# One attention-and-mixer kernel: v of the first batch placed in the mirror buffers, first loads spread by need, and one more batch fully mirrored by DMA

## The chip, the cores and the metric

One core of one Trainium2 chip. Times are device microseconds of a whole launch. A "span" is the profiled execution alone and is some 2 us shorter than the launch time of the same run. In the profiles PE is TensorE, PEld its weight loads, ACT ScalarE, DVE VectorE, POOL GpSimd and SPq the queue in which SyncE issues transfers; L396 is a line of the kernel.

## The reference, cut to what matters

```python
# B, S, D = 8, 3008, 256; z has 64 features
scores = (1 / S) * z @ z.T                 # symmetric in query and key
out    = maximum(scores, 0)**2 @ v
x      = u * out
h      = maximum(x.T @ w_tok1, 0) @ w_tok2   # token mixer, w_tok1 is 3008 x 256
y      = x + h.T
result = y + maximum(y @ w_ch1, 0) @ w_ch2   # channel mixer, 256 -> 1536 -> 256
```

Because scores are z times its own transpose, block (query q, key g) of the squared scores is the transpose of block (g, q). There are 6 x 6 blocks of 512 x 512 for each batch.

## The kernel before

A Python scheduler orders all instructions. TensorE computes score blocks ("sc"), ScalarE evicts them with a ReLU into one of six score buffers ("at"), VectorE squares them there, TensorE multiplies them with v ("acc"), VectorE gates with u into xT. The mixers follow ("a_ps", "h_ps", "hp", "op") and fill TensorE between attention blocks of the next batch. Batch 0 has no mixer work beside it.

A block that is not computed is a mirror: a DMA transpose of the score buffer into one of ten buffers "fl", issued from SyncE. The score buffer is free only when TensorE and that transpose have read it.

```python
def direct_block(b, q, g):           # computed on TensorE, not mirrored
    return b == 0 or g >= q or (b == 1 and g == 0)

def flips(b, q, g):                  # this computed block is also turned into (g, q)
    return g > q and not direct_block(b, g, q)

def flip(b, q, g, at, uses, done):
    fl = sb.tile([P, GK, QW], BF16, tag="fl", name="fl", bufs=ROOM["fl"])     # 10
    nc.sync.dma_start_transpose(
        out=fl.rearrange("p j (i s) -> p (j i) s", s=P), in_=at[:])
    blocks[b, g, q] = (done, fl[:, :, :], "fl", [1])
    release("at", uses, done.t)      # the score buffer: its last use may be the transpose
```

GpSimd issues the loads in program order, SyncE the transposes in program order; both stand still while the next one's buffer or data is not ready:

```python
def load_v(b, c):
    vt = sb.tile([P, GK, D], BF16, tag="v", name="v_sb", bufs=8)
    # ... (cut) one or three loads from GpSimd
def load_u(b, q):
    ur = sb.tile([P, QW // P, D], BF16, tag="ur", name="ur", bufs=2)
    # ... (cut) load from GpSimd
def turn_u(b, q):                    # uT, needed by the gate of block q
    # ... (cut) nc.sync.dma_start_transpose(out=uT, in_=ur)

# ... (cut) group n is the n-th attention block; v of the next batch near the end of this one
at_group(base + (NQ - 1) * NG - 2 + (j if j > 1 else 0), lambda b=b, c=c: load_v(b + 1, c))
for c in range(NG):
    at_group(NG - 1 + 4 * c, lambda c=c: load_w_tok1(c))
    at_group(NG + 1 + 4 * c, lambda c=c: load_w_tok2(c))
    at_group(NG + 4 + 4 * c, lambda c=c: order_w_tok2(c))
```

A group number orders the load in GpSimd's program.

Of the kernel before, what the change touches and what calls it, by code (L numbers as in the profile page):

```python
# [13 lines left out]
P = 128  # L14
# [4 lines left out]
class Done:  # L19


    def __init__(self, t=None):
        self.t = t


class Op:
# [16 lines left out]
def kernel(  # L43
# [100 lines left out]
                wp[:], zero[:, :P], zero[:], start=True, stop=True, skip_group_check=True)  # L144

    def load_v(b, c):
        vt = sb.tile([P, GK, D], BF16, tag="v", name="v_sb", bufs=8)
        n = full_tiles[c]
        nc.gpsimd.dma_start(out=vt[:, :n, :], in_=rows_of(v[b], c))  # L149
        if n < GK:  # L150
            for r in range(2):
                nc.gpsimd.dma_start(
                    out=vt[r * TAIL:(r + 1) * TAIL, n, :], in_=last_rows(v[b]))
        vs[b, c] = vt
        loading(LOAD)

    def load_u(b, q):
        ur = sb.tile([P, QW // P, D], BF16, tag="ur", name="ur", bufs=2)
        n = full_tiles[q]
        nc.gpsimd.dma_start(out=ur[:, :n, :], in_=rows_of(u[b], q))  # L160
        if n < QW // P:
            nc.gpsimd.memset(ur[TAIL:, n, :], 0.0)
            nc.gpsimd.dma_start(out=ur[:TAIL, n, :], in_=last_rows(u[b]))
        urs[b, q] = ur
        loading(LOAD)
# [18 lines left out]
        loading(LOAD)  # L184

    def load_w_tok2(c):
        st = sb.tile([P, DT, QW], BF16, tag="ws", name="ws", bufs=1)
        W = widths[c]
        nc.gpsimd.dma_start(
            out=st[:, :, :W],  # L190
            in_=moe_w_tok2.rearrange("(tc t) s -> t tc s", t=P)[:, :, c * QW:c * QW + W])
        ws[c] = st
        loading(LOAD)

    def order_w_tok2(c):
        st = ws.pop(c)
        W, n = widths[c], full_tiles[c]
        for h in range(DT):
            nc.gpsimd.tensor_copy(
                w_tok2_sb[:, h, c * QW:c * QW + n * P].rearrange("p (t s) -> p t s", s=P),  # L200
                st[:, h, :n * P].rearrange("p (s t) -> p t s", t=n))
        if n * P < W:
            nc.gpsimd.tensor_copy(
                w_tok2_sb[:, :, c * QW + n * P:c * QW + W], st[:, :, n * P:W])
# [18 lines left out]

    def direct_block(b, q, g):


        return b == 0 or g >= q or (b == 1 and g == 0)

    def flips(b, q, g):

# [286 lines left out]
    def finished(blk, g):  # L517
        blk.parts[g] -= 1
        if not blk.parts[g]:
            _, _, name, uses = blocks.pop((blk.b, blk.q, g))  # L520
            release(name, uses, pe[0] + 0.2)

    def block_ready(blk, g):
        e = blocks.get((blk.b, blk.q, g))
# [69 lines left out]
    def gate(blk, dh, t):  # L594
        b, q, W = blk.b, blk.q, blk.W
        acc = blk.acc[dh]
        uT = uTs[b, q]
        if dh == 0:
            xTs[b, q] = sb.tile([P, DT, QW], BF16, tag="xT", name="xT", bufs=ROOM["xT"])
            live["xT"] += 1  # L600
            live["x"] += 1
            if W < QW:
                nc.gpsimd.memset(xTs[b, q][:, :, W:], 0.0)
        xT = xTs[b, q]
        full, rest = W // P, W % P
        nc.vector.tensor_mul(  # L606
            xT[:, dh, :full * P].rearrange("p (t s) -> p t s", s=P),
            acc[:, :full * P].rearrange("p (t s) -> p t s", s=P),
            uT[:, :full, dh, :])
        if rest:  # L610
            nc.vector.tensor_mul(
                xT[:, dh, full * P:W], acc[:, full * P:W], uT[:, full, dh, :rest])
        if dh == DT - 1:
            push("sp", t, 1.25, 5.5, lambda t: turn_x(b, q, t), first=1)

    def turn_x(b, q, t):
        x = sb.tile([P, DT, QW // P, P], BF16, tag="x", name="x_sb", bufs=ROOM["x"])
# [19 lines left out]
    def add_mixer(b):  # L637
# [95 lines left out]
                release("xT", xT_uses[q])  # L733

        def ch2(q, half, i, end):
            if i == 0:
                take_slot()
                st["op"] = psum.tile([P, 2, D], F32, tag="ps", name="op", bufs=3)
            op = st["op"]
            n = full_tiles[q]  # L740
            both = half * 2 + i == n
            c0 = (half * 2 + i) * P
            for cc in range(CHT):
                if both:
                    h2 = pair["hs"][:, cc, :]
                else:
                    h2 = st["h2", q, cc // 2][:, cc % 2, c0:c0 + P]
                nc.tensor.matmul(  # L748
                    op[:, i, :], h2, w_ch2_sb[:, cc, :], start=(cc == 0 and i == 0),
                    stop=(cc == CHT - 1), skip_group_check=True)  # L750
            if i < pieces_of(q, half) - 1:
                return
            if half == halves(q)[1]:
                live["h2"] -= CHT // 2

            def residual(t):
                us = st["u", q]
                res = sb.tile([P, 2, D], F32, tag="res", name="res", bufs=3)
                if half * 2 + 1 < n:
                    nc.vector.tensor_add(  # L760
                        res.rearrange("p i (h d) -> p i h d", d=P),
                        op.rearrange("p i (h d) -> p i h d", d=P),
                        us[:, :, half * 2:half * 2 + 2, :].rearrange("p h i d -> p i h d"))
                    nc.sync.dma_start(
                        out=rows_of(out[b], q)[:, half * 2:half * 2 + 2, :],
                        in_=res[:])
                else:
                    k = half * 2
                    ends = [(0, slice(0, P), us[:, :, k, :], rows_of(out[b], q)[:, k, :])]
                    if i == 1:  # L770
                        lower, upper = slice(0, TAIL), slice(TAIL, P)
                        ends.append((1, lower, pair["ut"][:], last_rows(out[b - 1])))
                        ends.append((1, upper, us[upper, :, k + 1, :], last_rows(out[b])))
                    for j, r, u_rows, to in ends:
                        nc.vector.tensor_add(
                            res[r, j, :].rearrange("p (h d) -> p h d", d=P),
                            op[r, j, :].rearrange("p (h d) -> p h d", d=P), u_rows)
                        nc.sync.dma_start(out=to, in_=res[r, j, :])
                free["sp"] = max(free["sp"], t) + 0.4
                if half == halves(q)[1]:  # L780
                    live["us"] -= 1
            ring.append(push("dve", max(end + 0.21, known(st["turned", q])), 0.62, 0.75,
                             residual))
# [17 lines left out]
        def pieces_of(q, half):  # L801

            return 1 if q == NQ - 1 and half == 1 and b % 2 == 0 else 2

        def add_ch2(q, half, i):
            two = pieces_of(q, half) == 2
            tails.append(Piece(1.312, [h2_done[q, c2] for c2 in range(CHT // 2)] + w_done[2:],
                               lambda end: ch2(q, half, i, end), opens=two and i == 0,
                               closes=two and i == 1))

# [46 lines left out]

    vorder = [0, LAST] + list(range(1, LAST))
    new_zT(0)
    zero = sb.tile([P, QW], BF16, tag="ws", name="zero", bufs=1)  # L860
    nc.vector.memset(zero[:], 0.0)
    make_identity(nc, ident)
    zf0 = [first_z(c) for c in range(NG)]
# [24 lines left out]
    for b in range(B):  # L888
        base = b * NQ * NG
        for q in range(NQ):  # L890
            m = b * NQ + q + 2
            if m < B * NQ:
                at_group(base + q * NG + 2, lambda m=m: load_u(m // NQ, m % NQ))
                at_group(base + q * NG + 5, lambda m=m: turn_u(m // NQ, m % NQ))
        if b + 1 < B:
            held = {}

            def ask_z(b, c, held):
                held[c] = load_z(b + 1, c)

            at_group(base + 3 * NG, lambda b=b: new_zT(b + 1))
            for j, c in enumerate(vorder):
                at_group(base + 3 * NG + j, lambda b=b, c=c, h=held: ask_z(b, c, h))
                at_group(base + 3 * NG + j + 3, lambda b=b, c=c, h=held:
                         turn_next_z(b, c, h.pop(c)))
                at_group(base + (NQ - 1) * NG - 2 + (j if j > 1 else 0),
                         lambda b=b, c=c: load_v(b + 1, c))
    def turn_late_z(c):


# [16 lines left out]
        at_group(c - GK + 1, lambda c=c: turn_late_z(c))  # L927
    at_group(3, lambda: turn_u(0, 0))
    at_group(6, lambda: turn_u(0, 1))
    for c in range(NG):  # L930
        at_group(NG - 1 + 4 * c, lambda c=c: load_w_tok1(c))
        at_group(NG + 1 + 4 * c, lambda c=c: load_w_tok2(c))
        at_group(NG + 4 + 4 * c, lambda c=c: order_w_tok2(c))
    w_done = [Done() for _ in range(4)]

    def ask_w_ch(part):
        load_w_ch(part)
        w_done[part].t = pe[0] + 16.0

    for part in range(4):  # L940
        n = NG + 2 + 6 * part
        at_group(n, lambda part=part: ask_w_ch(part))

    per_batch = 0.87 * NQ * (2 + CHT // 2) + 1.35 * 4 * NQ
    flat = NQ * NG * 1.73 + NQ * (NQ + 1) / 2 * 0.63
# [130 lines left out]
```

## Time and profile before

| what | before |
|---|---|
| time, three runs | 1174.66 us (1174.34 to 1177.71) |
| its median in each of the five jobs of this record | 1174.5, 1172.22, 1172.69, 1172.89, 1173.0 |
| span; TensorE busy | 1170.1; 1162.0 us |
| score matmuls; groups of them in the timeline | 752; 130 |
| mirror transposes | 100 |

TensorE is the bound and has no gap above 0.21 us between 16 us and the last stage.

### The profile page before, as it was taken

How to read it: one execution, taken by the hardware profiler on the slowest of the kernel's cores; microseconds unless marked ns; L12 is line 12 of the kernel's file. 1: busy time of each engine (PE TensorE's matmuls, PEld its weight loads, DVE VectorE, ACT ScalarE, POOL GpSimd, SP SyncE). 2: the span in 40 equal slices, each digit the busy share in tenths (PEclk: the TensorE clock that was granted, in tenths of full speed). 3: DMA queues.
4: the chain of work that ended last, by engine and by line, in shares of the span. 5: the costliest groups of instructions: out<-in, count | busy, mean ns of one | idle time of the engine just before them, and what ended most of it. 6: DMA issues, size and time to landing. Idle time of an engine off the chain costs nothing.

```text
span 1170.1 us, 17839 instructions
## 1 busy us (share of the span) xinstructions
PE 1162.0 (99%) x7069; PEld 630.4 (54%) x7069; DVE 557.6 (48%) x836; ACT 523.4 (45%) x652; POOL 159.9 (14%) x328
## 2 busy tenths in 40 slices
PE   9999999999999999999999999999999999999998
PEld 3334455555546555464555655556454564555666
DVE  5776655355342653335534355332653337511544
ACT  7886644436342364434524245353544435433221
POOL 2561101200121110111101101011110110000000
PEclk9999999999999999999999999999999999999999
DMA  8997947989689985996969887798878989651232
GB/s 148 166 160 134 177 106 122 173 133 174 128 136 177 154 153 126 156 171 132 156 132 173 149 151 139 141 174 147 147 127 149 187 135 163 108 124 39 57 77 68
DMA packets 462339, 162.95 MB, mean 139 GB/s; under 512 B 426224, under 2 KB 439856, under 8 KB 462256
## 3 DMA queue, kind: packets, MB, share of 16 engines
q1 hardware_dynamic: 434400, 129.12, 59.0%
q0 software_dynamic: 27344, 32.32, 19.3%
q8 instruction: 55, 0.90, 0.3%
q10 hardware_dynamic: 512, 0.38, 0.1%
q14 instruction: 28, 0.23, 0.1%
HBM read 65.40 MB, written 24.64 MB: 77 GB/s over the span
## 4 chain that ended last, share of the span: by engine, by line
PE 97%; DMA 1%; DVE 1%; ACT 1%; issue 1%; SPq 0%; POOL 0%; DVEq 0%; ACTq 0%
PE acc L513 42%; PE op L748 21%; PE hp L707 21%; PE sc L379 7%; PE a_ps L653 4%; PE h_ps L670 3%; ACT at L417 1%; DMA zf<-in_z_dram 0%; DMA v_sb<-in_v_dram 0%; DVE xT L676 0%; DVE at L425 0%; DVE h2pre L722 0%; DVE xT L606 0%; SPq L120 0%; DVE res L760 0%
## 5 line engine op out<-in xcount | busy, mean ns | idle before, releaser
L417 ACT ACTIVATE at<-sc 128x1024 bf16<-128x1024 f32 (+1 forms) x294 | 280.9, 1023 | 205.2 <-PE sc L379 204.4
L513 PE MATMUL acc<-at,v_sb 128*128 128x512 bf16 (+2 forms) x1504 | 358.0, 378 | 0.6 <-DMA v_sb<-in_v_dram 0.5
L513 PEld LDWEIGHTS <-v_sb 128*128 128x128 bf16 (+1 forms) x2304 | 209.2, 97 | 268.2 <-issue 66.7
L720 ACT ACTIVATE h2pre<-hp 128x1024 bf16<-128x1024 f32 (+1 forms) x183 | 183.6, 1007 | 303.0 <-PE hp L707 300.3
L425 DVE TENSOR_TENSOR at<-at 128x1024 bf16<-128x1024 bf16 (+1 forms) x294 | 205.9, 708 | 170.3 <-ACT at L417 169.4
L707 PE MATMUL hp<-xT,w_ch_sb 128*128 128x512 bf16 (+1 forms) x1152 | 265.1, 375 | 0.0
L748 PE MATMUL op<-w_ch_sb,h2pre 128*128 128x256 bf16 x2208 | 258.4, 273 | 0.3 <-DVE xT L676 0.2
L748 PEld LDWEIGHTS <-h2pre 128*128 128x128 bf16 x2208 | 215.9, 98 | 46.2 <-issue 0.5
L513 PE MATMUL acc<-fl,v_sb 128*128 128x512 bf16 (+1 forms) x800 | 190.7, 371 | 0.2 <-DVE xT L606 0.2
L707 PEld LDWEIGHTS <-w_ch_sb 128*128 128x128 bf16 x1152 | 112.7, 98 | 126.7
L760 DVE TENSOR_TENSOR res<-op,u_sb 128x512 f32<-128x512 f32 x88 | 60.8, 691 | 209.2 <-PE op L748 206.2
L722 DVE TENSOR_SCALAR h2pre<-hp 128x1024 bf16<-128x1024 f32 (+1 forms) x105 | 126.5, 1205 | 54.3 <-PE hp L707 54.1
L606 DVE TENSOR_TENSOR xT<-acc,uT 128x512 bf16<-128x512 f32 (+1 forms) x96 | 63.3, 665 | 109.0 <-PE acc L513 108.7
L405 ACT ACTIVATE at<-sc 128x512 bf16<-128x512 f32 (+3 forms) x164 | 59.3, 447 | 87.5 <-PE sc L379 87.5
L379 PE MATMUL sc<-zT 64*128 64x512 bf16 (+1 forms) x752 | 97.8, 360 | 0.3
L453 DVE TENSOR_TENSOR at<-at 128x512 bf16<-128x512 bf16 (+3 forms) x164 | 47.0, 339 | 47.9 <-ACT at L405 47.9
L111 POOL COPY zr<-zs 128x512 bf16<-128x512 bf16 x42 | 26.5, 632 | 294.0 <-DMA zT<-zr 293.6
L379 PEld LDWEIGHTS <-zT 64*128 64x128 bf16 x752 | 32.0, 94 | 58.1 <-issue 40.0
L160 POOL DMA_DIRECT2D ur<-in_u_dram x48 | 25.9, 540 | 238.5 <-DMA uT<-ur 237.2
L676 DVE TENSOR_TENSOR xT<-xT,h_ps 128x1024 bf16<-128x1024 bf16 (+1 forms) x48 | 55.6, 1191 | 5.5 <-PE h_ps L670 5.5
L670 PE MATMUL h_ps<-w_tok_sb,a_sb 128*128 128x512 bf16 (+1 forms) x192 | 44.4, 374 | 0.1
L149 POOL DMA_DIRECT2D v_sb<-in_v_dram x48 | 25.9, 543 | 134.7 <-PE acc L513 134.5
(43 smaller groups left out, 228.1 us busy)
## 6 DMA issues: line engine op xcount, KB each, us to landing
out_dram<-res SPq DMA_DIRECT2D x88, 256.0 KB, 2.4
v_sb<-in_v_dram POOLq DMA_DIRECT2D x40, 256.0 KB, 4.9
ur<-in_u_dram POOLq DMA_DIRECT2D x40, 256.0 KB, 5.4
zs<-in_z_dram POOLq DMA_DIRECT2D x35, 64.0 KB, 4.5
at<-at SPq DMA_TRANSPOSE x123, 2.5
fl<-at SPq DMA_TRANSPOSE x100, 4.4
v_sb<-in_v_dram POOLq DMA_DIRECT2D x8, 192.0 KB, 7.3
w_ch_sb<-in_moe_w_ch_dram POOLq DMA_DIRECT2D x4, 384.0 KB, 5.7
```

The source lines that it names most:

```text
L379: nc.tensor.matmul(sc[:, r, c0:c1], zT[h, k * P:(k + 1) * P], zT[h, q * QW + c0:q * QW + c1], start=True, stop=True)
L405: nc.scalar.activation(a3[:, i, c0:c1], sc[:, r, c0:c1], ACT.Relu, scale=inv_S)
L417: nc.scalar.activation(view, sv, ACT.Relu, scale=inv_S)
L425: nc.vector.tensor_mul(view, view, view)
L513: nc.tensor.matmul(o, vs[blk.b, g][rows, i, dh * P:(dh + 1) * P], rhs, start=first, stop=stop, skip_group_check=True)
L606: nc.vector.tensor_mul(xT[:, dh, :full * P].rearrange("p (t s) -> p t s", s=P), acc[:, :full * P].rearrange("p (t s) -> p t s", s=P), uT[: ...
L670: nc.tensor.matmul(h[:, dh, :W], st["a"][:, th, dh * P:(dh + 1) * P], w_tok2_sb[:, th, q * QW:q * QW + W], start=(th == 0), stop=(th == 1))
L707: nc.tensor.matmul(hp[:, r, :W], w_ch1_sb[:, dc, cc * P:(cc + 1) * P], xT[:, dc, :W], start=(dc == 0), stop=(dc == DT - 1))
L720: nc.scalar.activation(h2[:, :, :W], hp[:, :, :W], ACT.Relu)
L722: nc.vector.tensor_single_scalar(h2[:, :, :W], hp[:, :, :W], 0.0, AX.max)
L748: nc.tensor.matmul(op[:, i, :], h2, w_ch2_sb[:, cc, :], start=(cc == 0 and i == 0), stop=(cc == CHT - 1), skip_group_check=True)
L760: nc.vector.tensor_add(res.rearrange("p i (h d) -> p i h d", d=P), op.rearrange("p i (h d) -> p i h d", d=P), us[:, :, half * 2:half * 2 + ...
```

## The change

Its intent: compute five score blocks less, in batch 1, and make room and DMA time for their mirrors. The core, with cuts marked:

```diff
 def load_v(b, c):
-    vt = sb.tile([P, GK, D], BF16, tag="v", name="v_sb", bufs=8)
+    if b == 0:
+        vt = sb.tile([P, GK, D], BF16, tag="fl", name="v_sb", bufs=ROOM["fl"])
+        live["fl"] += 1
+    else:
+        vt = sb.tile([P, GK, D], BF16, tag="v", name="v_sb", bufs=8)
 ... (cut)
-    ur = sb.tile([P, QW // P, D], BF16, tag="ur", name="ur", bufs=2)
+    ur = sb.tile([P, QW // P, D], BF16, tag="ur", name="ur", bufs=3)
 ... (cut: the staging tile of w_tok2 moves into the room of "h2")
-    return b == 0 or g >= q or (b == 1 and g == 0)
+    return b == 0 or g >= q
 ... (cut)
-    push("sp", t, 1.25, 5.5, lambda t: turn_x(b, q, t), first=1)
+    push("sp", t, 1.25, 7.5, lambda t: turn_x(b, q, t), first=1)
 ... (cut: the last pair of output pieces is added and stored in two halves)
-    tails.append(Piece(1.312, [h2_done[q, c2] for c2 in range(CHT // 2)] + w_done[2:],
+    needs = [Sooner(h2_done[q, c2], 0.218 * c2) for c2 in range(CHT // 2)]
+    tails.append(Piece(1.312, needs + w_done[2:],
 ... (cut)
+items = [lambda c=c: load_v(1, c) for c in vorder]
+items += [lambda c=c: load_w_tok1(c) for c in range(NG)]
+first_tok2 = len(items)
+items += [lambda c=c: load_w_tok2(c) for c in range(NG)]
+items += [lambda part=part: ask_w_ch(part) for part in range(4)]
+for k, item in enumerate(items):
+    n = NG - 2 + k * (NQ - 1) * NG // len(items)
+    at_group(n, item)
```

More of the change, by code (lines that the diff above doesn't have):

```diff
@@ L23, in __init__, with t @@
         self.t = t
+class Sooner:
+    def __init__(self, done, us):
+        self.done, self.us = done, us
+    @property
+    def t(self):
+        return None if self.done.t is None else self.done.t - self.us
 class Op:
@@ L186, in load_w_tok2 @@
     def load_w_tok2(c):
-        st = sb.tile([P, DT, QW], BF16, tag="ws", name="ws", bufs=1)
+        st = sb.tile([P, DT, QW], BF16, tag="h2", name="ws", bufs=ROOM["h2"])
         W = widths[c]
@@ L192, in load_w_tok2 @@
         ws[c] = st
+        live["h2"] += 1
         loading(LOAD)
@@ L196, in order_w_tok2 @@
         st = ws.pop(c)
+        live["h2"] -= 1
         W, n = widths[c], full_tiles[c]
@@ L521, in finished @@
             release(name, uses, pe[0] + 0.2)
+            if blk.b == 0 and blk.q == NQ - 1:
+                live["fl"] -= 1
     def block_ready(blk, g):
@@ L735, in ch2 @@
         def ch2(q, half, i, end):
-            if i == 0:
+            apart = alone(q, half)
+            if i == 0 or apart:
                 take_slot()
@@ L748, in ch2 @@
                 nc.tensor.matmul(
-                    op[:, i, :], h2, w_ch2_sb[:, cc, :], start=(cc == 0 and i == 0),
+                    op[:, i, :], h2, w_ch2_sb[:, cc, :], start=(cc == 0 and (i == 0 or apart)),
                     stop=(cc == CHT - 1), skip_group_check=True)
-            if i < pieces_of(q, half) - 1:
+            over = i == pieces_of(q, half) - 1 and half == halves(q)[1]
+            if over:
+                live["h2"] -= CHT // 2
+            if i < pieces_of(q, half) - 1 and not apart:
                 return
-            if half == halves(q)[1]:
-                live["h2"] -= CHT // 2
             def residual(t):
@@ L758, in residual @@
                 res = sb.tile([P, 2, D], F32, tag="res", name="res", bufs=3)
-                if half * 2 + 1 < n:
+                if not apart and half * 2 + 1 < n:
                     nc.vector.tensor_add(
@@ L768, in residual @@
                     k = half * 2
-                    ends = [(0, slice(0, P), us[:, :, k, :], rows_of(out[b], q)[:, k, :])]
-                    if i == 1:
+                    j = i if apart else 0
+                    ends = [(j, slice(0, P), us[:, :, k + j, :],
+                             rows_of(out[b], q)[:, k + j, :])]
+                    if both:
                         lower, upper = slice(0, TAIL), slice(TAIL, P)
@@ L779, in residual @@
                 free["sp"] = max(free["sp"], t) + 0.4
-                if half == halves(q)[1]:
+                if over:
                     live["us"] -= 1
@@ L803, in pieces_of, with alone @@
             return 1 if q == NQ - 1 and half == 1 and b % 2 == 0 else 2
+        def alone(q, half):
+            return pieces_of(q, half) == 1 or (b, q, half) == (B - 1, NQ - 1, 0)
         def add_ch2(q, half, i):
-            two = pieces_of(q, half) == 2
-            tails.append(Piece(1.312, [h2_done[q, c2] for c2 in range(CHT // 2)] + w_done[2:],
+            two = not alone(q, half)
+            needs = [Sooner(h2_done[q, c2], 0.218 * c2) for c2 in range(CHT // 2)]
+            tails.append(Piece(1.312, needs + w_done[2:],
                                lambda end: ch2(q, half, i, end), opens=two and i == 0,
@@ L859 @@
     new_zT(0)
-    zero = sb.tile([P, QW], BF16, tag="ws", name="zero", bufs=1)
+    zero = sb.tile([P, QW], BF16, tag="h2", name="zero", bufs=ROOM["h2"])
     nc.vector.memset(zero[:], 0.0)
@@ L905 @@
                          turn_next_z(b, c, h.pop(c)))
-                at_group(base + (NQ - 1) * NG - 2 + (j if j > 1 else 0),
-                         lambda b=b, c=c: load_v(b + 1, c))
+                if b:
+                    at_group(base + (NQ - 1) * NG - 2 + (j if j > 1 else 0),
+                             lambda b=b, c=c: load_v(b + 1, c))
     def turn_late_z(c):
@@ L929 @@
     at_group(6, lambda: turn_u(0, 1))
-    for c in range(NG):
-        at_group(NG - 1 + 4 * c, lambda c=c: load_w_tok1(c))
-        at_group(NG + 1 + 4 * c, lambda c=c: load_w_tok2(c))
-        at_group(NG + 4 + 4 * c, lambda c=c: order_w_tok2(c))
     w_done = [Done() for _ in range(4)]
@@ L938, in ask_w_ch @@
         w_done[part].t = pe[0] + 16.0
-    for part in range(4):
-        n = NG + 2 + 6 * part
-        at_group(n, lambda part=part: ask_w_ch(part))
+    items = [lambda c=c: load_v(1, c) for c in vorder]
[6 more added lines that the diff above has]
+        at_group(n, item)
+        if 0 <= k - first_tok2 < NG:
+            at_group(n + 4, lambda c=k - first_tok2: order_w_tok2(c))
     per_batch = 0.87 * NQ * (2 + CHT // 2) + 1.35 * 4 * NQ
```

## The prediction

> **What bounds the kernel now.** I read the engine totals first, then the stretches, then who makes TensorE wait, then the chain of work in order of time. The head of the page:
>
> ```profile
> span 1170.1 us, 17839 instructions
> PE 1162.0 (99%) x7069; PEld 630.4 (54%) x7069; DVE 557.6 (48%) x836; ACT 523.4 (45%) x652; POOL 159.9 (14%) x328
> PE acc L513 42%; PE op L748 21%; PE hp L707 21%; PE sc L379 7%; PE a_ps L653 4%; PE h_ps L670 3%; ACT at L417 1%; DMA zf<-in_z_dram 0%; DMA v_sb<-in_v_dram 0%; DVE xT L676 0%; DVE at L425 0%; DVE h2pre L722 0%; DVE xT L606 0%; SPq L120 0%; DVE res L760 0%
> ```
>
> PE is busy for 1162.0 of 1170.1 us, and 97% of the chain that ended last is PE work. A time can only fall here if PE gets fewer columns to stream, fewer changes of kind, or fewer gaps. The view of stretches shows where the 8.1 us without PE work lie:
>
> ```profile
> 0.00:10.00 10.00, 8.80 (x41) 3.33 (x41) 4.03 (x9) 6.41 (x8) 4.02 (x13) 1.00 0.75 141
> 10.00:20.00 10.00, 8.79 (x50) 3.09 (x49) 6.38 (x12) 6.75 (x8) 2.52 (x5) 1.00 0.98 175
> 80.00:100.00 20.00, 20.00 (x115) 8.05 (x112) 13.94 (x25) 17.45 (x20) 6.77 (x13) 1.00 1.18 190
> 100.00:120.00 20.00, 20.00 (x125) 10.68 (x124) 11.71 (x18) 8.86 (x13) 2.63 (x5) 1.00 0.66 110
> 1150.00:1170.00 20.00, 15.33 (x121) 11.55 (x119) 7.75 (x10) 3.14 (x4) 1.76 (x6) 0.98 0.18 57
> ```
>
> The first number after the length is PE's busy time: 2.4 us are missing in the first 20 us, 4.7 us in the last 20, and nothing at the passage from batch 0 to batch 1 (80 to 120 us), although the DMA share there reaches 1.18. The clock is 1.00. So **the loads that the change spreads hold up nothing now**: the longest wait of PE on a load is 0.5 us, on v at the start.
>
> **What the skill says.** "TensorE: Matmul & The Clock Gate", section "Wait — 56ns, not 53.3ns?", gives N/2.4 GHz plus about 2.5 ns per warm matmul, 215.7 ns for 512 columns. The trace agrees: one run of 24 matmuls of 512 columns took 5.18 us, 216 ns each. The mean of 378 ns in the groups is latency, not spacing. The same page, "Part 3: Packing small matmuls", lets matmuls on different rows of the array run together; six score matmuls (64 rows each) take 0.65 to 0.75 us, thus three pairs of 216 ns. "DMA: Bandwidth & Descriptors", section "Issuing engines are not separate DMA queues", says that all transfers share the same 16 engines, so mirror transposes and loads lengthen each other; the trace agrees in that the fl<-at transposes land after 4.4 us in the median, 11.0 at most.
>
> **The change, part by part.**
>
> 1. *Mirror blocks.* A score block (q,g) of batch 1 and its mirror (g,q) are transposes of one another. Before, key block 0 of batch 1 was computed directly for every query block, and nothing was mirrored into it. After, blocks (q,0), q = 1 to 5, are made by a DMA transpose of (0,q). Removed: 5 blocks of 2 units, a unit being a pair of concurrent matmuls with one ScalarE eviction (1028 ns) and one VectorE square (709 ns). Eight units have 512 columns, two 448: 8 x 0.2158 + 2 x 0.1892 = 2.10 us of PE. The groups must lose 20 score matmuls (752 to 732) and 10 evictions and 10 squares (294 to 284); ScalarE loses 10.1 us and VectorE 7.1 us, which pay nothing, at 45 and 48% of the span.
>
> 2. *Changes of kind.* Scores run in groups of three units between attention matmuls. The chain shows what a group costs:
>
> ```profile
> 59.31 0.75 PE sc L379 x6
> ...
> 63.51 2.69 PE acc L513 x12
> 66.20 0.76 PE sc L379 x6
> 66.96 3.02 PE acc L513 x14
> ```
>
> The six take 0.75 instead of 3 x 0.216 = 0.65, and the twelve 2.69 instead of 12 x 0.2158 = 2.59: about 0.1 us on entering and 0.1 on leaving the score kind. Ten units fewer are 3.3 groups fewer: 3.3 x 0.2 = 0.67 us, if the scheduler keeps its groups of three.
>
> 3. *What is added.* Five transposes of 512 KB into mirror buffers (100 to 105), each holding the issuing queue about 1.9 us (its median), some 10 us in all around 87 to 105 us. In that queue only uT (92.95) and x_sb (94.29) are issued between 81 and 104 us, so they fit. The mirrors read in later query blocks have tens of microseconds; only the one for (1,0) is needed within about 15. No PE work is added; I take 0.
>
> 4. *v of batch 0 in the mirror buffers, loads spread, a third u buffer.* Batch 0 mirrors nothing, so six of ten mirror buffers lend their room. The v of batch 1 can then load from the first query block on instead of at groups 28 to 35. GpSimd waits 134.5 us for attention matmuls before v loads and 237.2 us for transposes before u loads; some of these vanish, but PE never waits for the result. Worth 0 by themselves; they make part 1 safe.
>
> 5. *The end.* The last output piece pair is finished in two halves. Before, the end is
>
> ```profile
> 1162.64 2.78 PE L748 MATMUL op<-w_ch_sb,h2pre 128*128 128x256 bf16 x24
> ...
> 1165.46 0.69 DVE L760 TENSOR_TENSOR res<-op,u_sb 128x512 f32<-128x512 f32 x1 [1.41 <-PE op L748]
> 1166.18 0.34 SPq L764 DMA_DIRECT2D out_dram<-res  x1
> ```
>
> After, the last addition has 256 columns, which take 0.43 us in the same stage, so 0.26 us less; and its output is 128 KB, landing in 2.3 instead of 2.4 us: 0.1. Together 0.36 us. The first half adds while the second computes.
>
> 6. *Earlier starts of the second channel product (the scheduler now counts that its later inputs are needed later), and 7.5 instead of 5.5 us assumed for the x transpose.* Both only reorder PE work in the middle, where PE is always busy. I take 0, plus or minus about 1 us (five groups of 0.2 us more or fewer).
>
> Sum: 2.10 + 0.67 + 0.36 = 3.1 us. 1174.66 - 3.1 = 1171.5; I choose 1171.4.
>
> **Rivals.**
>
> *A new wait eats the gain.* Mirrors of batch 1 compete at 84 to 105 us with what remains of the loads, in a stretch whose DMA share is already above 1; the transpose of batch 0's last x, which its mixer needs, comes at the same time in the same queue. If x or the first mirror came 3 us late with nothing else ready, the time would be 1174 to 1175. Against it: v loads leave this stretch, six blocks of (1,0) attention are some 10 us of work to hide in, and batches 2 to 7 already live with the same mirrors without a PE gap. Chance about 0.1.
>
> *Only the columns count.* If the ten units vanish but as many groups remain, some of them shorter, the gain is 2.1 + 0.36 = 2.5 us: 1172.2.
>
> *Hidden stalls of batch 0 go as well.* PE matmul ends are modelled, and a few score groups lie stretched (at 39.19 six took 1.07 us where 0.75 is usual, waiting for ScalarE). If smoother loads or buffers removed several of these and start gaps, up to 3 us more could go: 1168.5. Against it: these waits are on ScalarE, VectorE and the first v, none of which the change relieves.
>
> *ScalarE or VectorE becomes the bound?* Both get less work; excluded.
>
> **Range and chances.** The certain part is 2.1 us; the rest is scheduling luck of about 1 us, and the three times before spread from 1174.34 to 1177.71, a median within perhaps 0.5 us. I take 1168.8 to 1173.8. 2% is 23 us: a gain of that size is impossible with 8 us of PE idleness and 2 us of work removed; a loss of it would need a broken pipeline. Faster 0.01, same 0.98, slower 0.01.
>
> **What would show it right or wrong.** Right: 732 score matmuls, 284 plain evictions, 105 fl<-at transposes, PE busy around 1159 and still 99%, three or four fewer score groups, a last VectorE addition of 0.43 us. Step 3 is wrong if PE waits appear at 95 to 135 us on a mirror or on x_sb. Step 4 is wrong if PE idleness at the start changes by more than 0.5 us, step 2 if the number of score groups does not fall, step 6 if PE busy changes much more than columns and groups explain. The total goes wrong if gaps open in batch 1, or if the reordering changes the number of groups in batches 2 to 7 by more than five.

## More of the kernel before

About one run in five of this kernel is 3 to 11 us longer, so one run in isolation decides nothing.

## The result, and the profile after

| | before | after |
|---|---|---|
| time, first comparison | 1174.5 us | 1175.54 us (1174.9 to 1176.66) |
| ratio | | 1.0007, 95% interval 0.9983 to 1.0031 |
| time, second comparison, another job | 1172.89 us | 1177.18 us (1175.64 to 1177.98) |
| ratio | | 1.003, 95% interval 1.0011 to 1.0049 |
| span | 1170.1 us | 1174.8 us |

A ratio is the mean time of one kernel's fast runs over that of the other's fast runs of the same rounds, so not quite the ratio of the medians. It is "the same" at 2%, but not the 3 us gain that was forecast: by the medians the changed kernel is 1 to 4 us slower, and the second interval excludes no change.

The counts came out as intended. From the changed kernel's page (groups with busy us and mean ns, and transposes with count and us to landing):

```profile
span 1174.8 us, 17791 instructions
L434 ACT ACTIVATE at<-sc 128x1024 bf16<-128x1024 f32 (+1 forms) x284 | 271.9, 1023 | 164.1 <-PE sc L396 158.7
L396 PE MATMUL sc<-zT 64*128 64x512 bf16 (+1 forms) x732 | 95.7, 362 | 0.3
fl<-at SPq DMA_TRANSPOSE x105, 4.6
```

732 score matmuls, 284 evictions, 105 mirrors. PE was busy for 1163.5 us here and for 1160.3 in a second trace without slow clock, where some 1159 were forecast. What was not intended is in the view of who makes TensorE wait (total us, times, longest):

```profile
PE acc L530 <- DVE xT L625: 3.8, 3, 2.4
...
PE a_ps L672 <- ACT at L434: 0.4, 1, 0.4
```

Two places hold them, as the view of stretches shows, of the kernel before and then of the changed one. The columns are the stretch, its length, busy us (and instructions) of PE, PEld, DVE, ACT, POOL, then granted clock, DMA share, GB/s:

```profile
20.00:40.00 20.00, 19.84 (x108) 7.52 (x106) 15.80 (x24) 17.66 (x20) 6.41 (x11) 1.00 0.93 154
95.00:130.00 35.00, 35.00 (x206) 16.43 (x206) 22.15 (x36) 22.16 (x29) 4.01 (x9) 1.00 0.82 140
```

```profile
20.00:40.00 20.00, 17.64 (x86) 6.47 (x85) 11.37 (x18) 14.27 (x17) 7.42 (x14) 0.91 1.11 190
95.00:130.00 35.00, 33.20 (x186) 15.42 (x184) 19.59 (x33) 18.38 (x25) 6.70 (x13) 0.95 1.21 191
```

TensorE lost 2.2 us in the first stretch and 1.8 in the second, and its clock fell in both.

**The gap at 25 us.** The chain of the changed kernel in order of time (start, us, what):

```profile
11.67 6.68 DMA ur<-in_u_dram
18.35 0.02 issue
18.36 8.19 DMA uT<-ur
...
26.65 0.70 DVE xT L625
27.35 0.04 issue
27.39 3.84 PE acc L530 x9
```

The first u transpose took 8.19 us to land. The gate needs it, and TensorE needs the gate to have emptied the accumulator. It waited 2.37 us, then ran nine matmuls in 3.84 us instead of 9 x 0.2158 = 1.94: the granted clock was 0.59 between 27 and 30 us. Loss: 2.37 + 1.90 = 4.3 us.

What was in its way stands in GpSimd's timeline, first of the changed kernel, then of the one before:

```profile
13.48 0.54 POOL L176 DMA_DIRECT2D ur<-in_u_dram  x1 [0.68 <-DMA v_sb<-in_v_dram]
14.81 0.53 POOL L165 DMA_DIRECT2D v_sb<-in_v_dram  x1 [0.80 <-DMA v_sb<-in_v_dram]
```

```profile
22.79 0.54 POOL L160 DMA_DIRECT2D ur<-in_u_dram  x1 [10.27 <-DMA uT<-ur]
```

Before, GpSimd stood for 10.27 us at the third u load, whose buffer the first u transpose had to free, and no later load could start. With a third buffer it went on and issued v of batch 1, needed 80 us later, right behind the u that was needed now. Between 18 and 22 us the DMA share was 0.56 before and 1.12 after, and the first u transpose, which took 8.2 us here, had landed after 3.0 us before.

**The stop at 105 us.** In the timeline of the changed kernel:

```profile
108.67 2.85 ACT L434 ACTIVATE at<-sc 128x1024 bf16<-128x1024 f32 x3 [3.97 <-DMA fl<-at]
...
109.75 1.03 PE L672 MATMUL a_ps<-x_sb,w_tok_sb 128*128 128x256 bf16 x8 [0.36 <-ACT at L434]
...
111.99 0.37 PE L530 MATMUL acc<-at,v_sb 64*128 64x512 bf16 x1 [1.21 <-DVE xT L625]
```

ScalarE waited 3.97 us for a score buffer that a mirror transpose was still reading. Its scores stayed in PSUM, and TensorE stood for 0.36 us, then 1.21 us for a gate that VectorE took after the late squares, then 0.22: 1.8 us. After it 40 matmuls of a_ps took 5.72 us instead of 40 x 0.1092 = 4.37 and four score matmuls 0.81 instead of 0.43. Loss: 1.8 + 1.7 = 3.5 us.

In sum: 1170.1 - 3.1 (the forecast gain) + 4.3 + 3.5 = 1174.8, the measured span. The agreement is closer than the terms deserve: for the second trace of the same kernel, with gaps of 3.5 and 3.4 us and no fall of the clock at either, the same sum gives 1173.9 against 1175.0.

### The profile page after: what moved, and what is told of

Same layout as the page of the kernel before. It is cut to its first block, busy times and chain, and to the rows that moved or that the text cites. A ratio compares the mean times of both kernels' runs of the same rounds, so it can differ in the third digit from the quotient of the medians.

```text
span 1174.8 us, 17791 instructions
## 1 busy us (share of the span) xinstructions
PE 1163.5 (99%) x7049; PEld 630.8 (54%) x7049; DVE 542.7 (46%) x819; ACT 521.5 (44%) x650; POOL 161.1 (14%) x328
## 4 chain that ended last, share of the span: by engine, by line
PE 95%; DMA 2%; DVE 1%; ACT 0%; issue 0%; POOL 0%; SPq 0%; ACTq 0%; DVEq 0%
PE acc L530 41%; PE op L768 21%; PE hp L726 21%; PE sc L396 6%; PE a_ps L672 4%; PE h_ps L689 3%; DMA uT<-ur 1%; DMA ur<-in_u_dram 1%; DMA fl<-at 1%; DMA zf<-in_z_dram 1%; ACT at L434 0%; DVE xT L695 0%; POOL v_sb L165 0%; DVE xT L625 0%; DVE h2pre L741 0%
## 5 line engine op out<-in xcount | busy, mean ns | idle before, releaser
L530 PE MATMUL acc<-at,v_sb 128*128 128x512 bf16 (+3 forms) x1464 | 352.4, 380 | 4.3 <-DVE xT L625 3.8
L739 ACT ACTIVATE h2pre<-hp 128x1024 bf16<-128x1024 f32 (+1 forms) x191 | 191.1, 1006 | 364.4 <-PE hp L726 362.5
L434 ACT ACTIVATE at<-sc 128x1024 bf16<-128x1024 f32 (+1 forms) x284 | 271.9, 1023 | 164.1 <-PE sc L396 158.7
L442 DVE TENSOR_TENSOR at<-at 128x1024 bf16<-128x1024 bf16 (+1 forms) x284 | 200.3, 713 | 177.9 <-ACT at L434 177.4
L530 PE MATMUL acc<-fl,v_sb 128*128 128x512 bf16 (+1 forms) x840 | 199.9, 371 | 0.0
L741 DVE TENSOR_SCALAR h2pre<-hp 128x1024 bf16<-128x1024 f32 (+1 forms) x97 | 117.3, 1209 | 52.4 <-PE hp L726 51.5
L672 PE MATMUL a_ps<-x_sb,w_tok_sb 128*128 128x256 bf16 x384 | 46.0, 277 | 0.4 <-ACT at L434 0.4
```

The costliest lines, as they stand in the source:

```text
L434: nc.scalar.activation(view, sv, ACT.Relu, scale=inv_S)
L442: nc.vector.tensor_mul(view, view, view)
L530: nc.tensor.matmul(o, vs[blk.b, g][rows, i, dh * P:(dh + 1) * P], rhs, start=first, stop=stop, skip_group_check=True)
L672: nc.tensor.matmul(st["a_ps"][:, th, :], w_tok1_sb[:, k, th * P:(th + 1) * P], x[:, :, i, :], start=(k == 0 and th == 0), stop=(k == KT - ...
L739: nc.scalar.activation(h2[:, :, :W], hp[:, :, :W], ACT.Relu)
L741: nc.vector.tensor_single_scalar(h2[:, :, :W], hp[:, :, :W], 0.0, AX.max)
```

## The experiments

My theory of the first trace was: the third u buffer with the early v loads makes the gap at 25 us (a brake was taken away), and the mirrors make the stop at 105 us. The rivals: chance from run to run, the third u load by itself, the lent buffers, the scheduler's part. All kernels gave correct results. The table adds up TensorE's gaps above 0.2 us in the profiled run of each; times are medians of six runs, the profiled one among them, and stand beside the kernel before in the same job. The column of 95 to 150 us holds two kinds of stop: the one of ScalarE behind a mirror, and a later one, at 118 to 139 us, where TensorE waits for the transpose that completes a diagonal score block within its own buffer (at<-at).

| kernel | mirrors into key block 0 | gap at 20-30 us | gaps at 95-150 us | time | before | ratio, 95% |
|---|---|---|---|---|---|---|
| changed, again | 5 | 3.5 | 3.4 | 1177.18 | 1172.89 | 1.003, 1.0011-1.0049 |
| ur_two | 5 | 0 | 1.3 | 1176.02 | 1172.22 | 1.0017, 0.999-1.0044 |
| late_start | 5 | 0 | 13.4 | 1188.17 | 1172.22 | 1.0123, 1.0096-1.015 |
| g0_direct | 0 | 2.8 | 0 | 1182.98 | 1172.22 | 1.0092, 1.0066-1.0117 |
| before_mirror | 5 | 0 | 4.6 | 1180.92 | 1172.22 | 1.0062, 1.0035-1.009 |
| late_turn | 5 | 0 | 17.0 | 1191.38 | 1172.69 | 1.0173, 1.0133-1.0214 |
| ur_two_turn | 5 | 0 | 4.2 | 1176.57 | 1172.69 | 1.0028, 1.0013-1.0042 |
| ur_two_few | 3 | 0 | 0.7 | 1173.25 | 1172.69 | 1.0004, 0.9989-1.002 |
| sched_only | 0 | 0 | 0 | 1173.08 | 1172.69 | 1.0014, 0.9988-1.0041 |
| ur_two_early | 5 | 0 | 5.9 | 1173.02 | 1172.89 | 1.0011, 0.998-1.0042 |
| few_early | 3 | 0 | 0 | 1171.58 | 1172.89 | 0.9994, 0.997-1.0018 |
| ur_two_g0 | 0 | 0 | 0 | 1174.69 | 1172.89 | 1.0007, 0.9986-1.0028 |
| wch_after | 5 | 0 | 3.1, all after 125 | 1176.08 | 1173.0 | 1.0024, 0.999-1.0057 |
| few4_early | 2 | 0 | 0 | 1173.26 | 1173.0 | 0.9991, 0.9962-1.002 |
| few_wch | 3 | 0 | 0 | 1171.92 | 1173.0 | 0.9977, 0.9952-1.0002 |

### The gap at 25 us: two u buffers, or a later start

```diff
-ur = sb.tile(..., name="ur", bufs=3)      # ur_two
+ur = sb.tile(..., name="ur", bufs=2)
```

> The changed kernel with two u buffers instead of three; every engine's order of instructions stays the same, only waits on buffers differ. Theory (a brake was taken away): GpSimd's load of the third u again waits for the first u transpose, so the v loads of batch 1 behind it come after it; the first u transpose lands some 4 us sooner and the 2.4 us gap of TensorE at 25 to 27 us goes, with the slow clock behind it (9 attention matmuls took 3.84 us instead of 1.94): 4.3 us faster than the changed kernel, about 1171.2. The stop at 109 to 112 us stays. Rival (the gap has to do with something else, as the order of TensorE or run-to-run chance): the gap stays and the time is within 1 us of 1175.5.

No instruction moved (each engine's order in the trace is that of the changed kernel), only the wait on the buffer came back, and the gap was gone: in the same view of stretches,

```profile
20.00:40.00 20.00, 19.84 (x107) 7.48 (x106) 14.90 (x23) 17.65 (x20) 9.04 (x17) 1.00 0.93 160
95.00:130.00 35.00, 33.67 (x197) 15.96 (x194) 20.07 (x31) 19.51 (x26) 2.63 (x5) 1.00 1.04 178
```

The profiled run took 1170.56 us, as the theory wants; the timed ones took 1174.38 to 1179.46. So the cause of the gap holds and the size of the gain does not: something else varies from run to run. The three slowest timed runs have a granted clock of 0.996 or 0.997, the profiled one 1.0; that is what stops with slow clock behind them would leave, but no trace of such a run was kept.

Two things here were not expected. The stop at 105 us, which was to stay, is gone: ScalarE waits for no mirror, although all five are there, and the 1.33 us left, at 118 us, is the wait for a diagonal block. The loads moved 0.91 MB between 88 and 108 us, against 2.07 and 1.75 in the two traces of the changed kernel. And a new small wait for the gate appears at 81 us (0.68 us). Such waits at 67 to 82 us come to 0.3 to 1.5 us in every kernel with two u buffers and spread loads except few_early; the changed kernel has none.

```diff
-n = NG - 2 + k * (NQ - 1) * NG // len(items)          # late_start, three u buffers kept
+n = NG + 3 + k * ((NQ - 1) * NG - 5) // len(items)
```

> The changed kernel with the spread loads beginning five groups later (behind the fourth u load instead of before it), three u buffers kept. Theory: the v loads of batch 1, 768 KB issued between 14.8 and 18.6 us, are what lengthens the first u transpose to 8.2 us; without them the gap at 25 us goes, about 4 us faster than the changed kernel. Rival: the third u load, issued at 13.5 us, is enough to delay it: the gap stays, at most 1 us shorter, and the time is within 1.5 us of the changed kernel. The stop at 109 us stays under both.

The gap was gone here too, with the third u load issued at 13.42 us but the first v of batch 1 only at 23.75 us. TensorE's order is the changed kernel's up to 101 us. So **it is the v loads, not the third u load**; the buffer merely let them pass. Both expectations missed the time: it rose by some 12 us, all of it behind the other stop, which the later loads had stretched to 12.0 us (13.4 with a wait of 1.4 us for a diagonal block).

A second trace of the changed kernel:

> The changed kernel once more, on the chip of the next three, for a second trace and direct comparison. If the two stops belong to the kernel and not to one run, both come back: a gap of 1.5 to 3.5 us at 25 to 28 us, and 1 to 6 us of gaps between 100 and 115 us; median 1175 to 1179, which is 3 to 6 us above the kernel before on this chip.

Both stops came back, 3.5 us and 3.4, but the 3.4 are two things. The mirror stop is 1.85 us of it (0.41, 1.21 and 0.23), as long as in the first trace, and the rest a diagonal block that came late:

```profile
124.32 1.11 PE L530 MATMUL acc<-at,v_sb 128*128 128x512 bf16 x3 [1.52 <-DMA at<-at]
```

All three traces with three u buffers and early v loads have the first gap (2.4, 3.5, 2.8 us), with the first u transpose landing after 8.2, 8.7 and 8.1 us; none of the other fourteen has the gap, and the transpose took 3.0 us in ur_two and 4.4 in late_start.

### The stop at 105 us: with and without the mirrors

```diff
-return b == 0 or g >= q                                 # g0_direct; ur_two_g0 with bufs=2 as well
+return b == 0 or g >= q or (b == 1 and g == 0)
```

> The changed kernel with key block 0 of batch 1 computed directly again (the mirrors undone, all else kept). Theory (five mirror transposes in a stretch where TensorE has only 12 us of attention work for them): the stop at 109 to 112 us (1.8 us of gap and some 1.7 us at slow clock) goes, 2.8 us of score work come back; the gap at 25 us stays. Together within 1.5 us of the changed kernel, about 1175. Rival (the stop comes from the v of batch 0 in the mirror buffers or from the load order): the stop stays and the time is about 2.8 us longer, 1178.

> The changed kernel with both suspected causes taken away: two u buffers and key block 0 of batch 1 direct. Theory (the third u buffer and the mirrors are the whole loss): no gap at 25 us, none between 95 and 125 us; with the same order as the kernel that had 1182.98 with three u buffers, so its two late stops at 633 and 866 us may come back. If they were chance, 1172 to 1174, equal to before; if they belong to this order of transposes, 1178 to 1180. Rival (something else in the change costs): a gap in the first 130 us remains.

Without the mirrors there is no stop between 95 and 150 us in either. The times were worse than expected for g0_direct: in its profiled run a z transpose held scores back for 2.1 us at 633 us and a residual's u transpose for 2.8 us at 866 us, in the transpose queue of SyncE. Of these one came back in ur_two_g0 (1.9 us at 632), the other did not. So this order of transposes has a weak spot in a middle batch; I did not find which of its parts makes it.

The mirrors alone, on the kernel before, with v in its own buffers and loads as before:

```diff
-return b == 0 or g >= q or (b == 1 and g == 0)          # before_mirror
+return b == 0 or g >= q
```

> The kernel before with the mirror part alone: v of batch 0 in its own buffers, loads as before. Theory (the mirror transposes themselves are the bound there): a stop of TensorE of 2 us or more appears between 95 and 115 us although the mirror buffers are all free, no gap at 25 us; 2.8 us less score work against 2 to 5 us of stop and slow clock: within 2 us of the kernel before, 1173 to 1177. Rival (the mirrors are harmless, and the lent buffers or spread loads made the stop): no stop, about 1171.7, 2.8 us faster than before.

The stop appears, 4.6 us, with all mirror buffers free and no gap at 25 us. So the lent buffers are not needed for it. It is worse than expected: 8.7 us slower than before in the medians. Its timeline:

```profile
107.65 2.85 ACT L417 ACTIVATE at<-sc 128x1024 bf16<-128x1024 f32 x3 [7.66 <-DMA fl<-at]
...
108.73 1.71 PE L653 MATMUL a_ps<-x_sb,w_tok_sb 128*128 128x256 bf16 x8 [4.06 <-ACT at L417]
```

### What sets its length: a theory that fell

In late_start the first mirror was issued only at 101.91 us, behind a u transpose for whose load SyncE waited 15.2 us. I took this head of the line for the cause and moved that u transpose:

```diff
-at_group(base + q * NG + 5, lambda m=m: turn_u(m // NQ, m % NQ))       # late_turn, ur_two_turn
+at_group(base + q * NG + (11 if m == NQ + 1 else 5), lambda m=m: turn_u(m // NQ, m % NQ))
```

> The late-start kernel (1188 us, a stop of TensorE of 12 us at 105 us) with one u transpose, that of query block 1 of batch 1, moved six groups back in the issuing order, behind the mirror transposes of query block 0. Theory (head of the line: the queue that issues transposes in order stood at this u transpose for 15.2 us waiting for its load, the first mirror stood ready behind it for 8 us and its score buffers were not given back): the first mirror is issued within 1 us of its square, the stop shrinks from 12 to 2 to 4 us, the time falls by 8 us or more, to 1176 to 1180. Rival (the rate of the mirror transposes, some 3 us each, sets the stop): the stop stays above 9 us and the time above 1185.

> The two-u-buffer kernel with the same u transpose moved back. In its profile the first mirror was issued at once and the stop was 1.3 us, in a run of 1170.6 us, while its five timed runs lay between 1174.4 and 1179.5 us. Theory (in those runs the u load came later and the mirrors stood behind it): the timed runs come together at 1170 to 1174 us. Rival (the spread comes from elsewhere, as the rate of the mirrors or later stages): median still 1175 or more and a spread of 4 us or more.

Both predictions of the theory failed; the rival was right. In late_turn the first mirror was issued at 92.21 us, some 10 us sooner, yet it landed only 18.5 us later, and the stop grew from 12.0 to 14.2 us (17.0 with a wait of 2.8 us for a diagonal block). The head of the line then was the x transpose, which waited for a small fill that GpSimd does behind its weight loads, and its issue alone lasted 7.97 us. The trace points to the DMA engines themselves, full with the last loads: between 92 and 98 us the packets of the loads' queue took 83.4% of the 16 engines. In late_turn ScalarE and TensorE stood like this:

```profile
118.77 2.86 ACT L434 ACTIVATE at<-sc 128x1024 bf16<-128x1024 f32 x3 [17.80 <-DMA fl<-at]
...
119.84 2.51 PE L672 MATMUL a_ps<-x_sb,w_tok_sb 128*128 128x256 bf16 x11 [14.20 <-ACT at L434]
```

Set beside each other, the traces give a simple law. ScalarE waited 3.97, 7.66, 15.60 and 17.80 us for a mirror (changed, before_mirror, late_start, late_turn); TensorE's stop on ScalarE behind it was 0.36, 4.06, 12.00 and 14.20 us. **The difference is 3.6 us each time**, and so it is in after_again (4.02 and 0.41), ur_two_turn (5.24 and 1.63) and ur_two_early (7.29 and 3.69). In the changed kernel TensorE had 4.7 us of work left when ScalarE stood still (104.70 to 109.39 us); less the eviction of 1.03 us for which it must wait in any case, that leaves 3.6.

### Fewer mirrors, and loads out of the way

```diff
-return b == 0 or g >= q                                 # ur_two_few: two u buffers, three mirrors
+return b == 0 or g >= q or (b == 1 and g == 0 and q < 3)
```

> The two-u-buffer kernel with mirrors for query blocks 3, 4, 5 of batch 1 only (blocks (1,0) and (2,0) direct again, so (0,1) and (0,2) are not mirrored): three transposes of 512 KB instead of five in query block 0. Score matmuls 740. Theory (too many mirrors for 12 us of attention work): no stop of TensorE over 0.5 us between 95 and 120 us, 1.7 us of the 2.8 us of score work still saved, timed median 1171 to 1173 with a spread under 3 us. Rival (head of the line alone matters, number of mirrors does not): median within 1 us of the two-u-buffer kernel, 1175 to 1177, with its spread.

No wait of ScalarE on a mirror is left, and no stop at 105 us (0.7 us on a diagonal block at 119). The median lies in the expected range, the spread (1170.83 to 1176.37) does not.

```diff
-n = NG - 2 + k * (NQ - 1) * NG // len(items)            # ur_two_early, few_early
+n = NG - 2 + k * ((NQ - 1) * NG - 7) // len(items)
```

> The two-u-buffer kernel with the spread loads ending seven groups earlier (over 23 groups instead of 30), TensorE, ScalarE and transposes in nearly the same order. Theory (mirror transposes and the last loads share the DMA engines: the more load bytes in flight between 88 and 108 us, the longer the stop: 0.9 MB with 1.3 us, 1.7 with 4.6, 2.8 with 13): the loads move less than 0.9 MB there, the gaps between 95 and 125 us shrink to 1.5 us or less in sum, timed median 1170 to 1173 where the two-u-buffer kernel had 1177, spread under 4 us. Rival (five mirrors alone fill the DMA there, whatever the loads do): gaps of 1.3 us or more, median 1175 or more.

Inconclusive. Four timed runs were 1170.93 to 1173.30, the profiled one 1178.51 and one more 1181.76. In the profiled one the loads still moved 1.40 MB between 88 and 108 us, since three z transposes in a row held their queue for 14.90 us at 69 us and GpSimd stood behind them. The condition of the test was not met there.

> Candidate: two u buffers, mirrors for query blocks 3, 4, 5 only, loads ending seven groups earlier. Three mirrors were 1173.25 with a stop of 0.7 us at 119 us. Theory of shared DMA engines: the last stop goes too, 1.7 us of score work saved: 1170 to 1172, 1 us or more below the kernel before. Rival: other stops (a z transpose came 1.5 us late at 489 us) decide: 1172 to 1175.

> Two u buffers, mirrors for query blocks 4 and 5 only, loads ending seven groups earlier; three mirrors gave 1171.58. Both theories: no stop near 105 us. Score work saved is about 1.1 us instead of 1.7: 1171.5 to 1173. If it is faster than three mirrors by more than 1 us, the order in later batches decides and not the saved score work.

With three mirrors and this order five of six runs were 1171.07 to 1173.57, the sixth 1178.02; two mirrors give 1173.26, above the expected range. There is no stop between 95 and 150 us in either.

```diff
 n = NG - 2 + k * (NQ - 1) * NG // len(items)            # wch_after (5 mirrors), few_wch (3)
+if k >= first_tok2 + NG:
+    n = NQ * NG + 4 + k - first_tok2 - NG
```

> The two-u-buffer kernel with the four channel-weight loads (1.5 MB) moved behind the mirrors, to query block 1 of batch 1. Theory (mirrors and loads together overfill the DMA): between 88 and 108 us the loads move 0.9 MB or less in the profiled run; gaps of TensorE between 95 and 115 us of 0.5 us or less; timed median 1172 or less if the later weights hold nothing up (1176 if they do, with the gap then after 125 us). Rival (five mirrors alone suffice): a gap of 1 us or more between 95 and 115 us even so, median 1174 or more.

Five mirrors, and no gap between 95 and 115 us. ScalarE waited for a mirror for 3.43 us, just inside the 3.6:

```profile
104.50 2.85 ACT L434 ACTIVATE at<-sc 128x1024 bf16<-128x1024 f32 x3 [3.43 <-DMA fl<-at]
```

So, as in ur_two's profiled run, five mirrors do not make the stop by themselves: what else is in flight counts. But the gain was not to be had either: with the channel weights late, gaps came after 125 us (3.1 us) and one of 1.6 us at 909 us. The expected 0.9 MB of loads was missed (1.65 MB), so bytes in that stretch are a poor measure; when they come counts.

> Three mirrors, loads at the changed kernel's pace, channel weights behind the mirrors. Theory (shared DMA): no gap over 0.5 us between 95 and 115 us, 1170.5 to 1172.5. Rival (the later weights or later batches decide): 1173 or more.

Three mirrors with the same late weights has the lowest ratio of all: 1171.11 to 1172.32, against 1171.7 to 1180.23 of before in the same rounds. Its ScalarE never waits for a mirror, and its two stretches are as full as those of before (1.3 us of gaps lie between them, at 67 and 81 us):

```profile
20.00:40.00 20.00, 19.84 (x108) 7.45 (x106) 14.82 (x23) 17.66 (x20) 9.27 (x18) 1.00 0.96 159
95.00:130.00 35.00, 35.00 (x206) 16.34 (x206) 22.40 (x36) 21.92 (x30) 3.21 (x6) 1.00 1.00 174
```

It is 1.1 us faster than before in the medians; the interval of the ratio just reaches 1, so a gain is likely and not shown.

### The scheduler's part alone

`sched_only` is the kernel before with 7.5 us for the x transpose, the earlier allowed starts (`Sooner`) and the split last pieces; nothing else of the change is in it.

> The kernel before with the scheduler's part of the change alone: earlier allowed starts of the second channel product, 7.5 us assumed for the x transpose, the last pieces finished apart. Buffers, loads and mirrors as before. My step said 0 plus or minus 1 us, and 0.36 us less at the end: 1171 to 1173 against 1172.2. Rival (this reordering opens stops in the middle batches, as the 2.1 and 2.8 us ones at 633 and 866 us that appeared with key block 0 direct): 3 us or more slower than before, with stops of over 1 us behind the transposes in the middle.

1173.08 against 1172.69, with 130 score groups as before and no gap above 0.23 us after 17 us (one of 1.25 us, for a z transpose, at 13): this part neither gained nor lost anything that six runs resolve (the interval is -1.4 to +4.8 us). The rival of new stops in middle batches falls for this part.

## Why the prediction was wrong, point by point

- **Mirror blocks, counts and work (step 1): right.** 732, 284 and 105 as forecast. That the work is really saved is shown indirectly: the profiled run of ur_two had a span of 1168.6 us, 1.5 below before, with 2.0 us of gaps that before does not have. The second trace of the changed kernel has PE busy for 1160.3 us, 1.7 below before and some 1 us above the forecast.
- **Changes of kind (step 2): right in the count.** 127 groups in both traces of the changed kernel where before has 130. That this is worth 0.67 us is not shown by itself.
- **The five transposes (step 3): wrong, the first failing step.** "No PE work is added; I take 0" and "so they fit" looked at SyncE's order of issue. The transposes fit there; in the DMA engines beside the last loads they did not land in time, and a score buffer stays taken until its mirror has landed. The prediction itself said that mirrors and loads lengthen each other, and did not carry it into this step. Measured: a wait of ScalarE of 3.97 us, of which 0.36 reached TensorE at once and 1.4 through VectorE, so 1.8 us of gaps in the first trace (1.85 in the second, and 1.5 for a diagonal block), and 1.7 us of slow clock in the first.
- **v lent, loads spread, third u buffer (step 4): wrong, the second failing step.** "Worth 0 by themselves" counted GpSimd's waits of 134.5 and 237.2 us as idle time that costs nothing. Ten of those microseconds were the only thing that kept loads for later out of the way of the first u. Measured: 4.3 us in the first trace, 3.5 us in the second. That the lent buffers cost nothing agrees with the runs, but was not tested alone: before_mirror has the stop without them, and ur_two_g0, which keeps them, has no gap above 0.2 us between 17 and 67 us.
- **The end (step 5): right for the addition, the rest not seen.** The last addition is 0.42 us on 256 columns instead of 0.69. From its end to the end of the span 3.9 us pass in both kernels; the 0.1 us of the smaller store does not show.
- **The reordering (step 6): nothing against it.** sched_only is 0.4 us above before in the medians, inside the plus or minus 1 us of the step; six runs do not resolve 1 us.
- **The rivals.** "A new wait eats the gain", given 0.1, was the right one; I made it depend on x or the first mirror being late for their own use. x did come late (issued at 99.70 us and landed 6.6 us later, where before it was issued at 94.29 and took 5.4), and still TensorE never waited for it. It is the score buffer behind the mirror that was late. The reason I gave against it, "six blocks of (1,0) attention are some 10 us of work to hide in", counted work that itself needed those buffers: what was left to hide a wait of ScalarE was 3.6 us. The forecast range was too narrow mainly because this rival had too little weight.
- **What stays open.** Which loads in flight at which moment stretch a mirror from 4.4 to 18.5 us, what makes the diagonal blocks late, the stop in the middle batches of g0_direct, and why the clock fell after one gap and not after another. Several variants also shift the order that the scheduler gives TensorE (late_start from 102 us on, g0_direct from 97, wch_after from 106); ur_two and ur_two_early do not.

## What to carry to other kernels

A wait on a buffer can be the brake that keeps a queue in order of need; before adding a buffer, ask which transfers behind that wait will now run, and beside what. A DMA that reads a working buffer holds it until it lands, so its cost is that buffer's return and not its own bytes: compare the engine's wait for the buffer with the work its consumer still has in hand. Put transfers where other work can hide them: in this stretch three mirrors stopped TensorE behind ScalarE in none of three traces, five in seven of nine. A gain in time over the kernel before was not resolved for either.

## What the Trainium skill lacked or had wrong

- "TensorE: Matmul & The Clock Gate", section "Back-to-back issue gap", gives some 131 ns for each matmul of 512 columns in a sustained stream of weight loads and matmuls, and calls 216 ns too high. Here 24 of them with a weight load each took 5.18 us, 216 ns; the formula of the same page fits this, the 131 ns do not.
- The same page, section "What's actually happening", ties the slow clock to an idle window of about 3.4 us, free-running. Here a gap of 2.37 us, shorter than that window, was followed by a granted clock of 0.59 between 27 and 30 us, and a gap of 3.53 us of the same kernel by no fall. In g0_direct the clock was 0.58 and 0.57 in the 4 us behind gaps of 2.11 and 2.77 us and 1.00 behind one of 2.82. A cost of 0 to 1.9 us behind a gap is what the two runs of the changed kernel show.
- "TensorEngine Tiling (Array Packing)", section "Key Properties", says that a change of tiling mode drains TensorE, without a figure. Here changing from full-height matmuls to pairs of 64 rows and back took about 0.1 us each way, an estimate from the chain shown in the prediction (six score matmuls in 0.75 us instead of 0.65, twelve others in 2.69 instead of 2.59).
- "DMA: Bandwidth & Descriptors", section "DMA Transpose (X-bar)", has no figure for a transpose beside loads. The same transpose between buffers in SBUF, 512 KB, landed after 4.4 us in the median of the kernel before, and after 18.5 us in late_turn, where the packets of the loads took 83.4% of the engines.
